# First tile in 256-column halves, weight sums spread over later tiles, four marks moved from ScalarE to VectorE

## The chip, the cores and the metric

The kernel runs on one core of a Trainium2 chip. The metric is the device time of one execution in microseconds; three executions of the kernel before took 225.99, 226.69 and 230.72 us, so the median is 226.69 us. A difference of 2% of that is 4.5 us.

Five engines work side by side, each through its own list of instructions in a fixed order: TensorE (PE for the matmuls, PEld for the weight load that goes ahead of each matmul), VectorE (DVE), ScalarE (ACT), GpSimd (POOL) and SyncE (SP), which issues nearly all DMAs.

## The reference

A recurrent attention with a decaying state, followed by a bilinear feed-forward layer:

```
for t in range(S):
    state = gamma * state + einsum('bhd,bhe->bhde', k[:, :, t], v[:, :, t])
    y[:, :, t] = scale * einsum('bhd,bhde->bhe', q[:, :, t], state)
x = y.transpose(0, 2, 1, 3).reshape(B * S, H * D)
out = ((x @ w_a) * (x @ w_b)) @ w_out
```

B = 4, H = 8, S = 768, D = 64, so there are 3072 tokens of 512 channels; w_a and w_b are 512 x 1536, w_out is 1536 x 512. All inputs and the output are float32; the kernel multiplies in bfloat16 and sums in float32.

## The kernel before

The 3072 tokens are 24 slots of 128 tokens. TILES = [4, 2, 2, 2, 2, 4, 4, 4] groups them into eight tiles J = 0 to 7 of 512 or 256 tokens for the feed-forward part. For each tile there are twelve blocks ft = 0 to 11, one for each 128 of the 1536 hidden channels: `ffn_a` (L574) multiplies x by w_a in four matmuls (kt = 0 to 3) into a PSUM bank, ScalarE copies it to `asb` (L586), `ffn_g` (L588) does the same with w_b, and VectorE multiplies the two into `ht` (L597). A matmul of a block is as wide as the tile, 512 or 256 columns, except where `parts` (L568) cuts it into two halves. The three PSUM banks of the pool psff (tag "ff") go round among a, g, the outputs o and one half of the state products.

Then comes the output product. For J below 5, `ffn_out` (L621) does one 128-token slot i in twelve matmuls of 512 columns, and ScalarE copies the bank to `osb` (L634). For J = 5, 6, 7, `ffn_fast` (L667) does two slots at once with seven products of six 256-column matmuls in place of eight; it needs sums of w_out's quarters (`wt_bf`, made once for each sixth j of w_out by `combine_o`, L213: four VectorE instructions and a ScalarE cast, L217 to L221) and sums of ht's quarters (`hsum`, made by VectorE in `add`, L644, as the blocks go by).

The attention of slots 0 to 5 is done at the start. That of slots 6 to 23 is put in between as visits, by the table `ahead` (L815): at (J, ft) ahead of a block, or at (J, "o", i) ahead of an output product. A visit `turn(new, old)` (L397) does, on TensorE, the first half of `inter` for the old pair of slots (y from the carried state, L360), the chunk states of the new pair (L288), their scores (L318), the second half of `inter`, and `intra` (y from the masked scores, L372). That is up to 128 small matmuls of 64 columns, each with a weight load, so up to 256 instructions. `casts(t)` (L247) scales k and q of a slot on POOL, turns them with a DMA transpose into kqT, and asks for the loads of later slots. VectorE adds the chunk states to running sums (L302) and masks the scores (L324); ScalarE casts the sums to `gst` and, later, y to `xt` (L387).

Between the two halves of `inter` stands a mark: `fenced` (L335) puts a tiny copy of one column on an engine, which waits for the last matmul of the first half; the matmuls that write the same bank's other rows wait for the mark (`into`, L341). In the kernel before the mark of every turn is on ScalarE.

The order of each engine's list is the order in which the code is written (`seq` ties each instruction to the one before it on its engine). No planner changes it. The code of TensorE's list is itself brought onto the core while the kernel runs, in packets that the trace shows on a DMA queue of its own (q8).

Of the kernel before, what the change touches and what calls it, by code (L numbers as in the profile page):

```python
# [24 lines left out]
def kernel(  # L25
# [10 lines left out]
    nc = tc.nc  # L36
# [7 lines left out]
    NFT = DFF // P  # L44
# [288 lines left out]
    fence = {}  # L333
# [60 lines left out]
                seq(nc.vector.tensor_tensor(dst[:, s, on], src[:, s, on], part[:, s], op=ALU.add))  # L394
                seq(nc.vector.tensor_copy(dst[:, s, off], src[:, s, off]))

    def turn(new, old):  # L397
        catch_up()
        apart = None
        if old is not None:  # L400
            ys[old] = [psat.tile([P, 2, KT, D], F32, tag=f"y{c}", name="y") for c in range(2)]
            if new is None:
                both = psat.tile([P, 2, 2, KT, D], F32, tag="at", name="apart")
                apart = [both[:, c] for c in range(2)]
            inter(old, True, ys[old] if new is not None else apart)
# [168 lines left out]
    def ffn_a(J, ft, c0=0, c1=None):  # L574
        c1 = TILES[J] * P if c1 is None else c1
        if J not in ht:
            ht[J] = htp.tile([P, NFT, 4 * P], BF16, tag="ht", name="ht")
        fs = slice(ft * P, (ft + 1) * P)
        a = psff.tile([P, 4 * P], F32, tag="ff", name="a")[:, : c1 - c0]
        for kt in range(KT):  # L580
            for b0, b1 in parts(J, ft, c0, c1, 5):
                seq(nc.tensor.matmul(a[:, b0 - c0 : b1 - c0], wa_bf[:, kt, fs], xcols(J, kt, b0, b1),  # L582
                                     start=(kt == 0 and b0 == c0), stop=(kt == KT - 1 and b1 == c1),
                                     skip_group_check=True))
        asb = asbs[J, ft, c0] = asbp.tile([P, 4 * P], BF16, tag="asb", name="asb")[:, : c1 - c0]
        seq(nc.scalar.copy(asb, a))  # L586

    def ffn_g(J, ft, c0=0, c1=None):  # L588
        c1 = TILES[J] * P if c1 is None else c1
        fs = slice(ft * P, (ft + 1) * P)  # L590
        g = psff.tile([P, 4 * P], F32, tag="ff", name="g")[:, : c1 - c0]
        for kt in range(KT):
            for b0, b1 in parts(J, ft, c0, c1, 5):
                seq(nc.tensor.matmul(g[:, b0 - c0 : b1 - c0], wb_bf[:, kt, fs], xcols(J, kt, b0, b1),  # L594
                                     start=(kt == 0 and b0 == c0), stop=(kt == KT - 1 and b1 == c1),
                                     skip_group_check=True))
# [216 lines left out]
    for j in range(NO):  # L813
# [5 lines left out]
        (1, "o", 1): [(turn, 8, 6), (casts, 10)],  # L819
# [3 lines left out]
        (4, "o", 1): [(turn, 16, 14), (casts, 19)], (5, 0): [(casts, 20)],  # L823
        (5, 2): [(casts, 21)], (5, 8): [(turn, 18, 16), (casts, 22)],
        (5, "o", 2): [(turn, 20, 18), (casts, 23)],
# [63 lines left out]
```

## Time and profile before

| what | value |
|---|---|
| executions | 225.99, 226.69, 230.72 us, median 226.69 |
| the profiled execution's own time | 226.69 us |
| its span | 225.0 us (the other 1.69 us lie around it) |
| TensorE matmuls | busy 214.5 us, 95% of the span, 2717 of them |
| weight loads | busy 140.6 us |
| VectorE, ScalarE, GpSimd | busy 128.7, 98.0 and 81.8 us |
| granted TensorE clock | 0.997 on the mean of the span |
| idle of TensorE put down to "issue" | 1.4 us once (L631) and 1.7 us once (L664) |

TensorE's busy time is an overlapped one: matmuls are pipelined, a 512-column matmul is listed with 379 ns and a 256-column one with 273 ns, while four of 512 columns follow each other in 0.86 us. The chain of waits shows the pace, since it counts each piece only until the next one starts. "issue" in a view means that an engine stood still while nothing that the profile shows was being waited for.

### The profile page before, as it was taken

What the parts mean: (1) busy time and instruction counts of PE and PEld (TensorE: products, weight loads), DVE (VectorE), ACT (ScalarE), POOL (GpSimd) and SP (SyncE); (2) the same over time, 40 slices, a digit from 0 to 9 for tenths busy, and PEclk for the clock granted to TensorE, in tenths of its full rate; (3) what the DMA queues carried; (4) which work ended last, traced back from release to release, by engine and by line L of the source; (5) the groups of instructions that cost most, each with busy time, mean ns of one, the idle gap of its engine ahead of it and who ended that gap; (6) DMA issues with size and microseconds to landing.
All of it is one profiled execution on the core that took longest, in us unless ns stands there. A gap on an engine that the chain in (4) does not pass through costs nothing.

```text
span 225.0 us, 6583 instructions
## 1 busy us (share of the span) xinstructions
PE 214.5 (95%) x2717; PEld 140.6 (62%) x2717; DVE 128.7 (57%) x282; ACT 98.0 (44%) x225; POOL 81.8 (36%) x107
## 2 busy tenths in 40 slices
PE   8799999999999999997999999996999999999993
PEld 7578645784557867864885445476545478444582
DVE  2783547649895434470467267974457793256641
ACT  3674253443656426452447432724435442333331
POOL 6567798573653535161443526161000000000000
PEclk9999999999999999999999999999999999999998
DMA  6999999896998899999948987797200002200022
GB/s 180 345 379 382 365 317 407 249 213 141 217 251 183 224 210 188 212 170 249 215 102 200 212 199 164 170 272 170 93 0 4 0 3 96 93 0 1 3 93 93
DMA packets 94829, 39.74 MB, mean 177 GB/s; under 512 B 76112, under 2 KB 91728, under 8 KB 94800
## 3 DMA queue, kind: packets, MB, share of 16 engines
q1 hardware_dynamic: 94656, 39.20, 68.4%
q8 instruction: 21, 0.34, 0.6%
q10 hardware_dynamic: 144, 0.13, 0.2%
q14 instruction: 8, 0.07, 0.1%
HBM read 28.31 MB, written 6.29 MB: 154 GB/s over the span
## 4 chain that ended last, share of the span: by engine, by line
PE 79%; DMA 7%; issue 3%; DVE 3%; ACT 2%; POOL 2%; SPq 2%; DVEq 0%; ACTq 0%; POOLq 0%
PE a L582 25%; PE g L594 25%; PE o L664 12%; PE o L631 10%; DMA qf<-in_q_dram 4%; DMA vf<-in_v_dram 2%; POOL kqb L240 2%; DMA kqT<-kqb 1%; PE y L360 1%; DVE ht L597 1%; PE y L372 1%; PE at L318 1%; DVE hsum L654 1%; PE tp L440 1%; PE y L519 1%
## 5 line engine op out<-in xcount | busy, mean ns | idle before, releaser
L597 DVE TENSOR_TENSOR ht<-g,asb 128x256 bf16<-128x256 f32 (+1 forms) x98 | 53.9, 550 | 67.2 <-PE g L594 52.6
L594 PE MATMUL g<-xt,wb_bf 128*128 128x256 bf16 (+1 forms) x404 | 77.8, 318 | 0.2 <-ACT asb L586 0.2
L582 PE MATMUL a<-xt,wa_bf 128*128 128x256 bf16 (+1 forms) x404 | 77.5, 318 | 0.1
L586 ACT CAST asb<-a 128x256 bf16<-128x256 f32 (+1 forms) x98 | 46.2, 472 | 66.5 <-PE a L582 65.2
L594 PEld LDWEIGHTS <-wb_bf 128*128 128x128 bf16 x404 | 39.4, 98 | 22.9 <-issue 0.5
L582 PEld LDWEIGHTS <-wa_bf 128*128 128x128 bf16 x404 | 39.2, 98 | 22.7 <-DVE xt L201 0.4
L240 POOL TENSOR_TENSOR kqb<-kf,ktab 128x512 bf16<-128x512 f32 x21 | 22.5, 1072 | 39.9 <-DMA kf<-in_k_dram 36.2
L631 PE MATMUL o<-wo_bf,ht 128*128 128x512 bf16 x144 | 32.6, 379 | 1.4 <-issue 1.4
L240 POOL TENSOR_TENSOR kqb<-qf,qtab 128x512 bf16<-128x512 f32 x21 | 22.7, 1084 | 5.9 <-DMA qf<-in_q_dram 5.8
L631 PEld LDWEIGHTS <-ht 128*128 128x128 bf16 x144 | 13.6, 98 | 17.0 <-issue 1.7
L201 POOL CAST vb<-vf 128x512 bf16<-128x512 f32 x24 | 15.3, 646 | 17.0 <-DMA vf<-in_v_dram 7.5
L302 DVE TENSOR_TENSOR sums<-st,sums 128x256 f32<-128x256 f32 x30 | 12.7, 424 | 5.6 <-PE st L288 4.3
L664 PEld LDWEIGHTS <-hsum 128*128 128x128 bf16 x144 | 14.0, 98 | 2.1 <-DVE hsum L654 0.4
L634 ACT COPY osb<-o 128x512 f32<-128x512 f32 x12 | 7.0, 586 | 15.2 <-PE o L631 12.2
L664 PE MATMUL o<-wt_bf,hsum 128*128 128x256 bf16 x108 | 12.9, 273 | 0.2 <-DVE hsum L654 0.2
L664 PEld LDWEIGHTS <-ht 128*128 128x128 bf16 x108 | 10.4, 97 | 4.3 <-issue 1.9
L199 ACT CAST gst<-sums 128x256 bf16<-128x256 f32 x33 | 11.8, 412 | 0.1
L324 DVE TENSOR_TENSOR aT<-at,mask 128x512 bf16<-128x512 f32 x18 | 11.8, 680 | 0.0
L664 PE MATMUL o<-wo_bf,ht 128*128 128x256 bf16 x72 | 9.1, 273 | 1.7 <-issue 1.7
L387 ACT CAST xt<-y 128x512 bf16<-128x512 f32 x16 | 8.6, 592 | 4.2 <-PE y L372 4.2
L654 DVE TENSOR_TENSOR hsum<-ht 128x512 bf16<-128x512 bf16 (+1 forms) x24 | 9.1, 391 | 0.2
L201 POOL CAST wo_bf<-wsto 128x1024 bf16<-128x1024 f32 x6 | 6.2, 1040 | 3.2 <-DMA wsto<-in_moe_w_out_dram 3.2
(85 smaller groups left out, 171.1 us busy)
## 6 DMA issues: line engine op xcount, KB each, us to landing
out_dram<-osb SPq DMA_DIRECT2D x11, 512.0 KB, 3.2
kf<-in_k_dram SPq DMA_DIRECT2D x18, 256.0 KB, 4.0
qf<-in_q_dram SPq DMA_DIRECT2D x36, 128.0 KB, 3.9
vf<-in_v_dram SPq DMA_DIRECT2D x18, 256.0 KB, 4.3
wsta<-in_moe_w_a_dram SPq DMA_DIRECT2D x6, 512.0 KB, 7.6
wstb<-in_moe_w_b_dram SPq DMA_DIRECT2D x6, 512.0 KB, 7.9
wsto<-in_moe_w_out_dram SPq DMA_DIRECT2D x6, 512.0 KB, 9.0
kf<-in_k_dram SPq DMA_DIRECT2D x3, 512.0 KB, 6.2
```

The source lines that it names most:

```text
L199: seq(nc.scalar.copy(dst, src))
L201: seq(engine.tensor_copy(dst, src))
L240: seq(eng.tensor_tensor(dst, src, tab, op=ALU.mult))
L302: seq(nc.vector.tensor_tensor(new, u[c][:, s], old, op=ALU.add))
L324: unmasked.append(lambda r=r: seq(nc.vector.tensor_tensor(aT[n][:, r].rearrange("p s h d -> p (s h) d"), at[:, r].rearrange("p s h d -> p ...
L582: seq(nc.tensor.matmul(a[:, b0 - c0 : b1 - c0], wa_bf[:, kt, fs], xcols(J, kt, b0, b1), start=(kt == 0 and b0 == c0), stop=(kt == KT - 1 a ...
L586: seq(nc.scalar.copy(asb, a))
L594: seq(nc.tensor.matmul(g[:, b0 - c0 : b1 - c0], wb_bf[:, kt, fs], xcols(J, kt, b0, b1), start=(kt == 0 and b0 == c0), stop=(kt == KT - 1 a ...
L597: seq(nc.vector.tensor_tensor(ht[J][:, ft, c0:c1], g, asbs.pop((J, ft, c0)), op=ALU.mult))
L631: seq(nc.tensor.matmul(o, ht[J][:, ft, i * P : (i + 1) * P], wo_bf[:, f, 2 * r : 2 * r + 2, :].rearrange("p a d -> p (a d)"), start=(ft == ...
L654: seq(nc.vector.tensor_tensor(s[which], x(), y(), op=op))
L664: seq(nc.tensor.matmul(R[:, :DH], lhs, (wo_bf, wt_bf)[w][:, f, m, :], start=(first and f == 0), stop=(f == NH - 1), skip_group_check=True))
```

## The change

Four things are changed.

1. `parts` is called with NFT (12) in place of 5. In tile 0 the blocks 2 to 4 were in 256-column halves before; now blocks 2 to 11 are. This makes 7 blocks x 2 products x 4 = 56 more matmuls and as many weight loads, 112 more TensorE instructions, all ahead of the first visit. TensorE's list has 5,548 rows now in place of 5,436.
2. `combine_o` of the six parts of w_out stood after the output products (0,0) twice, (0,1), (0,2), (0,3) and (1,0); now it stands after (0,0), (0,1), (0,2), (0,3), (2,0) and (3,1).
3. The mark of the turns 8, 10, 16 and 20 is on VectorE in place of ScalarE.
4. Turn 22 stands ahead of block (6, 8) in place of (6, 6).

```
-            for b0, b1 in parts(J, ft, c0, c1, 5):
+            for b0, b1 in parts(J, ft, c0, c1, NFT):          (in ffn_a and in ffn_g)
...
-    def turn(new, old):
+    def turn(new, old, eng=nc.scalar):
...
-                fence[old, 0] = fence[old, 1] = fenced(nc.scalar)
+                fence[old, 0] = fence[old, 1] = fenced(eng)
...
-        (2, 2): [(casts, 11)], (2, 7): [(casts, 12)], (2, "o", 1): [(turn, 10, 8), (casts, 13)],
+        (2, 2): [(casts, 11)], (2, 7): [(casts, 12)], (2, "o", 1): [(turn, 10, 8, D_), (casts, 13)],
...
-        (6, 6): [(turn, 22, 20)], (6, "o", 0): [(turn, None, 22)],
+        (6, 8): [(turn, 22, 20)], (6, "o", 0): [(turn, None, 22)],
...
-    combined = {(0, 0): (0, 1), (0, 1): (2,), (0, 2): (3,), (0, 3): (4,), (1, 0): (5,)}
+    combined = {(0, 0): (0,), (0, 1): (1,), (0, 2): (2,), (0, 3): (3,), (2, 0): (4,), (3, 1): (5,)}
```

Three places show what moves. The first is TensorE's list around row 4,025 (counted from 0). Before, the last matmul of the second-last product of the first `ffn_fast` of tile 5 and the first instructions of turn 20 stand there (rows 4,021 to 4,025; o is the output bank, ht the hidden values, y the attention output, gst the carried state):

```order
L664 LDWEIGHTS ht_2792
L664 MATMUL o_3147<-wt_bf_175,ht_2792 128x256
L360 LDWEIGHTS gst5_161
L360 MATMUL y_3200<-kqT_2587,gst5_161 64x64
L360 LDWEIGHTS gst5_161
```

In the changed kernel the rows 4,025 to 4,029 are the end of an a product and the start of a g product in a block of tile 5:

```order
L582 LDWEIGHTS wa_bf_172
L582 MATMUL a_3164<-xt_2646,wa_bf_172 128x512
L594 LDWEIGHTS wb_bf_173
L594 MATMUL g_3171<-xt_2646,wb_bf_173 128x512
L594 LDWEIGHTS wb_bf_173
```

From the first visit on every instruction stands 112 rows further down the list; turn 22 has in addition changed places with the blocks 6 and 7 of tile 6 (32 rows). Counted in rows, the turns 12, 14, 16, 18 and 20 start at 2,467, 2,963, 3,227, 3,619 and 4,023 before, and at 2,579, 3,075, 3,339, 3,731 and 4,135 now. Nine rows of either list, the same nine places, wait for two semaphores at once.

The second place is VectorE's list from turn 8 to turn 10 (mark is the mark, sums the running state sums, aT the masked scores, the four rows L217 to L220 one `combine_o`; -: before, +: now):

```order
+L337 COPY mark<-bq 128x1
+L302 TENSOR_TENSOR sums<-st,sums 128x256 x4
+L324 TENSOR_TENSOR aT<-at,mask 128x512 x2
+L597 TENSOR_TENSOR ht<-g,asb 128x256 x12
 L217 TENSOR_TENSOR tmp<-wsto 128x256
 L218 TENSOR_TENSOR tmp<-wsto,tmp 128x256
 L219 TENSOR_TENSOR wt_bf<-wsto 128x256
 L220 TENSOR_TENSOR wt_bf<-wsto,tmp 128x256
-L302 TENSOR_TENSOR sums<-st,sums 128x256 x4
-L324 TENSOR_TENSOR aT<-at,mask 128x512 x2
-L597 TENSOR_TENSOR ht<-g,asb 128x256 x12
+L337 COPY mark<-bq 128x1
```

One `combine_o` that stood ahead of turn 8's work stands after the blocks of tile 2 now, directly ahead of turn 10's mark, and both marks are new in this list.

The third place is ScalarE's list at the end of tile 3, from the last cast of turn 12's sums over the two output copies (osb) to the copies of tile 4's blocks (asb):

```order
 L199 CAST gst_160<-sums 128x256
 L634 COPY osb<-o 128x512 x2
+L221 CAST wt_bf<-tmp 128x512
 L586 CAST asb<-a 128x256 x12
```

A `combine_o` cast stands between the last output copy of tile 3 and the first copy of tile 4 now.

More of the change, by code (lines that the diff above doesn't have):

```diff
@@ L580, in ffn_a @@
         for kt in range(KT):
-            for b0, b1 in parts(J, ft, c0, c1, 5):
+            for b0, b1 in parts(J, ft, c0, c1, NFT):
                 seq(nc.tensor.matmul(a[:, b0 - c0 : b1 - c0], wa_bf[:, kt, fs], xcols(J, kt, b0, b1),
@@ L592, in ffn_g @@
         for kt in range(KT):
-            for b0, b1 in parts(J, ft, c0, c1, 5):
+            for b0, b1 in parts(J, ft, c0, c1, NFT):
                 seq(nc.tensor.matmul(g[:, b0 - c0 : b1 - c0], wb_bf[:, kt, fs], xcols(J, kt, b0, b1),
@@ L818 @@
         (0, "o", 3): [(casts, 9, "kq"), (casts, 8, "v"), (casts, 9, "v")],
-        (1, "o", 1): [(turn, 8, 6), (casts, 10)],
-        (2, 2): [(casts, 11)], (2, 7): [(casts, 12)], (2, "o", 1): [(turn, 10, 8), (casts, 13)],
+        (1, "o", 1): [(turn, 8, 6, D_), (casts, 10)],
+        (2, 2): [(casts, 11)], (2, 7): [(casts, 12)], (2, "o", 1): [(turn, 10, 8, D_), (casts, 13)],
         (3, 0): [(casts, 14)], (3, 6): [(casts, 15)], (3, "o", 0): [(turn, 12, 10), (casts, 16)],
         (4, 0): [(casts, 17)], (4, "o", 0): [(turn, 14, 12), (casts, 18)],
-        (4, "o", 1): [(turn, 16, 14), (casts, 19)], (5, 0): [(casts, 20)],
+        (4, "o", 1): [(turn, 16, 14, D_), (casts, 19)], (5, 0): [(casts, 20)],
         (5, 2): [(casts, 21)], (5, 8): [(turn, 18, 16), (casts, 22)],
-        (5, "o", 2): [(turn, 20, 18), (casts, 23)],
-        (6, 6): [(turn, 22, 20)], (6, "o", 0): [(turn, None, 22)],
+        (5, "o", 2): [(turn, 20, 18, D_), (casts, 23)],
+        (6, 8): [(turn, 22, 20)], (6, "o", 0): [(turn, None, 22)],
     }
```

## The prediction

> **What bounds the kernel now.** I read the page first, then the chain of waits, then who TensorE waited for, then the timeline around the waits. From the page:
>
> ```profile
> span 225.0 us, 6583 instructions
> PE 214.5 (95%) x2717; PEld 140.6 (62%) x2717; DVE 128.7 (57%) x282; ACT 98.0 (44%) x225; POOL 81.8 (36%) x107
> ```
>
> TensorE is the bound: an edit counts only where it removes or makes a wait of TensorE, or changes its pace. The pace stands in the chain of waits, in pieces counted to the start of the next:
>
> ```profile
> 19.66 1.75 PE a L582 x16
> 30.44 0.86 PE a L582 x4
> ...
> 98.79 2.48 PE o L631 x11
> 101.27 1.41 issue
> ...
> 151.41 0.21 PE y L360 x10
> ...
> 152.63 0.98 PE o L664 x8
> 153.61 1.69 issue
> ```
>
> Halves go at 1.75 / 16 = 0.1094 us each, full matmuls at 0.86 / 4 = 0.215. And there are two pieces in which TensorE does nothing, named "issue": 1.41 and 1.69 us, together 3.10 us. The waits of TensorE name them as its two longest, with nothing else above 1.1 us:
>
> ```profile
> PE o L664 <- issue: 1.7, 1, 1.7
> PE o L631 <- issue: 1.4, 1, 1.4
> PE tp L440 <- DVE kqb L240: 1.1, 4, 0.4
> ...
> PE at L318 <- DMA kqT<-kqb: 0.2, 1, 0.2
> ```
>
> What "issue" is here: the page has a queue of 21 packets, 0.34 MB, so 16 KB each. TensorE's 2717 matmuls and 2717 weight loads make 5,434 instructions, 5,434 / 21 = 259 per packet. The first gap ends at row 2,747 of TensorE's list, the second at row 4,281; the list in between holds two rows that wait for two semaphores and so take an extra wait instruction each, and 1,534 + 2 = 1,536 = 6 x 256. So code comes in pages of 256 instructions, and both gaps end exactly at a page's first instruction. In both a page packet was on its way shortly before:
>
> ```profile
> q8 instruction: 21, 0.34, 0.6%
> q8 instruction: 1, 0.02, 13.4%
> q8 instruction: 1, 0.02, 5.8%
> 97.30 0.32 PE L360 MATMUL y<-kqT,gst 64*64 64x64 bf16 x16
> 98.29 0.51 PE L372 MATMUL y<-aT,vb 64*64 64x64 bf16 x32
> 102.69 2.97 PE L631 MATMUL o<-wo_bf,ht 128*128 128x512 bf16 x13 [1.41 <-issue]
> 155.30 0.60 PE L664 MATMUL o<-wo_bf,ht 128*128 128x256 bf16 x4 [1.69 <-issue]
> ```
>
> (The second and third rows are the windows 99 to 99.5 and 152.5 to 153.7 us.) A turn runs its 256 instructions from 97.30 to about 98.7 us, 5.6 ns each, against 0.1094 / 2 = 55 ns in a block. I read it so: when TensorE enters a page, the one after it is asked for; where a page starts at the beginning of a turn, it is used up too fast. In turn 12 a page starts 25 rows in (row 2,492), in turn 20 2 rows in (row 4,025), by 256 rows back from the gaps. These points are at about 97.4 us (the first of the turn's rows at 97.30 covers 32) and 151.4 us (the row of turn 20's first matmuls). To the ends of the gaps at 102.69 and 155.30 are 5.3 and 3.9 us: a next page takes that long.
>
> [...]
>
> **The change part by part.** The sum is made against the profiled execution, 226.69 us (span 225.0 us and 1.69 around it), which is also the median of the runs.
>
> *112 more instructions ahead of the visits.* All page starts fall 112 rows earlier in the work. I counted them through the changed list. Turn 12 now has a page start 168 rows in, turn 20 146 in, and before the next page over 160 rows of blocks or products follow the turn: at 55 ns that is 8.8 us against 5.3. Both gaps go: -1.41 - 1.69 = **-3.10**. What is late next there: nothing that the waits of TensorE name before the marks below.
>
> New short pages: the shortest distances of the changed list, timed by today's trace over the same work, are turn 14 to turn 16 (a page start near the beginning of `intra` in both), turn 18 into the blocks behind it (5.0 us), and tile 4's blocks into turn 14 (5.0 us). For the first:
>
> ```profile
> 116.90 0.50 PE L372 MATMUL y<-aT,vb 64*64 64x64 bf16 x31
> 121.05 0.46 PE L372 MATMUL y<-aT,vb 64*64 64x64 bf16 x32
> 116.20 0.44 PE L288 MATMUL st<-vb,kqb 64*64 64x64 bf16 x30
> 120.02 0.32 PE L360 MATMUL y<-kqT,gst 64*64 64x64 bf16 x16
> ```
>
> 121.05 - 116.90 = 4.15 us. In the kernel before, the page that starts in the L288 row (116.2) had its next one start at the end of the L360 row of turn 16 (16 matmuls from 120.02, some 0.13 us), 3.9 us later, and no "issue" wait of TensorE stands there. So a page takes between under 3.9 and 5.3 us: a wait of 0 to 1.15 us at turn 16, 0 to 0.3 at each of the two others. I take 0.5 for the three, nearer the pages without a wait: **+0.50** (0 to 1.75).
>
> *The halves themselves.* One a or g product is 8 x 0.1094 = 0.875 us in place of 0.86, times 14 = +0.21 us. The weight loads are hidden as they are in the row at 19.66 us, which is the same shape. Behind it, turn 8 waits for a transpose in any case:
>
> ```profile
> 62.80 3.29 DMA kqT<-kqb
> ...
> 66.13 0.32 PE at L318 x16
> ```
>
> The transpose lands at 62.80 + 3.29 = 66.09 us and the scores start then; a later start of TensorE is taken up there, if the DMA does not move. I take **+0.10** (0 to 0.21).
>
> *Marks on VectorE.* In the turns 10 and 16 TensorE waits for ScalarE's mark, which is queued behind an output copy:
>
> ```profile
> 83.59 0.21 PEld L360 LDWEIGHTS <-gst 64*64 64x64 bf16 x16 [0.17 <-ACT mark L337]
> 120.90 0.21 PEld L360 LDWEIGHTS <-gst 64*64 64x64 bf16 x16 [0.17 <-ACT mark L337]
> 80.30 0.42 DVE L597 TENSOR_TENSOR ht<-g,asb 128x256 bf16<-128x256 f32 x1 [0.45 <-PE g L594]
> 83.32 1.34 DVE L302 TENSOR_TENSOR sums<-st,sums 128x256 f32<-128x256 f32 x3 [2.60 <-PE st L288]
> ```
>
> Both go: **-0.34**. Queued behind the mark on VectorE are the sums, which wait for TensorE's later matmuls anyway. In turn 10 a `combine_o` (next rows) stands ahead of the mark: 0.506 + 0.642 + 0.415 + 0.484 = 2.05 us, inside the 2.60 us in which VectorE is idle: from 80.30 + 0.42 = 80.72 to 82.77, half a microsecond ahead of the sums at 83.32. If that cover is gone, TensorE waits for what is over. Turn 8 is held by the transpose, turn 20 shows no wait for its mark: 0 each.
>
> *Weight sums spread.* Work that leaves tiles 0 and 1 gains nothing, since no wait of TensorE names VectorE or ScalarE there. What arrives: the two `combine_o` at tiles 2 and 3.
>
> ```profile
> L217 DVE TENSOR_TENSOR tmp<-wsto 128x256 f32<-128x256 f32 x6 | 3.0, 506 | 0.0
> L218 DVE TENSOR_TENSOR tmp<-wsto,tmp 128x256 f32<-128x256 f32 x6 | 3.9, 642 | 0.2
> L219 DVE TENSOR_TENSOR wt_bf<-wsto 128x256 bf16<-128x256 f32 x6 | 2.5, 415 | 0.0
> L220 DVE TENSOR_TENSOR wt_bf<-wsto,tmp 128x256 bf16<-128x256 f32 x6 | 2.9, 484 | 0.0
> L221 ACT CAST wt_bf<-tmp 128x512 bf16<-128x512 f32 x6 | 3.6, 620 | 0.5 <-DVE tmp L218 0.4
> 105.69 0.59 ACT L634 COPY osb<-o 128x512 f32<-128x512 f32 x1 [2.00 <-PE o L631]
> 106.18 0.37 ACT L586 CAST asb<-a 128x256 bf16<-128x256 f32 x1
> 106.80 0.60 PE L594 MATMUL g<-xt,wb_bf 128*128 128x256 bf16 x4
> ```
>
> At the end of tile 3 ScalarE goes from the output copy straight to the first copy of tile 4, 106.18 to 106.55 us. The cast of 0.62 us now goes between (about 0.5 in a row of overlapping instructions), so that copy ends near 107.1. The fourth product of tile 4 (106.80) takes the bank that this copy frees, and waits about 0.3 us: **+0.30** (0 to 0.6). At (2,0) the cast stands ahead of a turn and a 2.7 us output product, which hide it. No DMA moves: SyncE's list is the same.
>
> *Turn 22 two blocks later.* VectorE has fewer blocks for its sums and masks before tile 6's hsum are due. The same place in tile 5 has one more sum, and cost TensorE this:
>
> ```profile
> 148.42 1.59 PE L664 MATMUL o<-wt_bf,hsum 128*128 128x256 bf16 x13 [0.17 <-DVE hsum L654]
> ```
>
> In tile 6 the last turn's matmuls and two products stand ahead, so I take **+0.10** (0 to 0.3).
>
> Sum: -3.10 + 0.50 + 0.10 - 0.34 + 0.30 + 0.10 = -2.44; 226.69 - 2.44 = 224.25, so **224.2 us**, 1.1% faster. That is inside 2%, about what a measurement of this kernel can tell from no change.
>
> **The rivals.**
>
> *The gaps come back elsewhere* (0.20). All three short pages take the 5.3 us of turn 12: 1.75 in place of 0.50, 225.5 us. For it: turn 12 did take that long. Against: the page of 3.9 us without a wait at the same place.
>
> *The gaps are not the code's* (0.08) but belong to the products in which they stand: then they stay, and -2.44 + 3.10 = +0.66, 227.3 us. For it: the profile only says "issue". [...] Against: the 1,536 instructions between them, and that only one of the 12 output products of L631 and one of the six fast ones has such a gap.
>
> *The weight loads of the halves stand open* (0.05), the side slower than before. 56 more loads, listed with 98 ns each:
>
> ```profile
> L582 PEld LDWEIGHTS <-wa_bf 128*128 128x128 bf16 x404 | 39.2, 98 | 22.7 <-DVE xt L201 0.4
> ```
>
> If all of it showed, 56 x 0.098 = 5.5 us, 224.2 + 5.5 = 229.7 us; it is slower than before from 2.44 / 56 = 44 ns a load on. It would be in tile 0, from 30 to 48 us. Against: 16 halves in 1.75 us, where an open load would give 16 x 0.2 = 3.3.
>
> *More is gained* (0.07): no short page waits, ScalarE's cast is hidden and the halves are free: -3.10 - 0.34 = -3.44, 223.25, and with the fastest of the three runs of before, 0.70 below the median, as the scatter, 222.6 us.
>
> **How the numbers follow.** My forecast has 0.60; its own range is 223.3 to 225.2 (its terms at their near ends). The range to hold 8 in 10 takes in the gain at its fullest with scatter, 222.6, and the short pages with ScalarE's wait at its full 0.6 and 0.7 of scatter, 225.5 + 0.3 + 0.7 = 226.5. Over 2% faster is under 222.2 us: 0.04, from the last rival. Over 2% slower is over 231.2 us: 0.02, beyond even the open loads. Within 2%: 0.94.
>
> **What would show it.** No "issue" piece over 0.3 us in the chain at the output product behind turn 12 or in the first fast product behind turn 20; the page packets 112 rows earlier. Any new "issue" piece stands in turn 16, within 40 rows behind turn 18 or in turn 14, and at a page's first row. Tile 0's blocks at 1.75 us for 16 halves. No wait for a mark in turns 10 and 16. A wait of some 0.3 us at tile 4's fourth product. I am wrong if the two gaps stay at their products, if a gap of over 1.2 us stands elsewhere, or if TensorE begins to wait for kqT in turn 16.

## The result and the profile after

The changed kernel took 224.44 us at the median of 20 executions, the kernel before 226.47 us at the median of 20 executions beside it. The ratio is 0.9913, with a 95% interval of 0.9884 to 0.9941: 0.9% faster, within the 2% that count as no change. The profiled execution of the changed kernel took 223.94 us with a span of 222.2 us; that of before 226.69 and 225.0 us.

From the page of the changed kernel, the span, the busy time of the engines, and the queue that brings TensorE's code:

```profile
span 222.2 us, 6684 instructions
...
PE 212.8 (96%) x2764; PEld 145.5 (65%) x2773; DVE 129.8 (58%) x286; ACT 97.3 (44%) x221; POOL 81.9 (37%) x107
...
q8 instruction: 21, 0.34, 0.6%
```

56 more weight loads are listed (2,773 in place of 2,717), and still the span is 2.8 us shorter. Whom TensorE waited for in the changed kernel (us in total, times, longest):

```profile
PE tp L440 <- DVE kqb L240: 1.8, 3, 1.4
...
PE o L631 <- issue: 0.6, 4, 0.2
PE y L360 <- issue: 0.6, 1, 0.6
...
PE y L360 <- DVE mark L337: 0.3, 1, 0.3
```

The two rows of before with 1.7 us (L664) and 1.4 us (L631) are gone; what is left of "issue" at L631 is four short waits of at most 0.2 us. A new "issue" of 0.6 us stands in a turn (y, L360), and so does a wait for a mark on VectorE. The chain of waits of the changed kernel shows the same at two of the places. Each row is a start, a length up to the next step, and what ran:

```profile
98.71 5.14 PE o L631 x23
...
119.34 0.15 PE y L360 x15
119.49 0.56 issue
120.06 0.21 PE y L360
```

The third place, the first fast product behind turn 20, stands in the timeline (start, length, engine and line, operation; an idle time ahead of a row would stand behind it in brackets):

```profile
151.47 1.49 PE L664 MATMUL o<-wo_bf,ht 128*128 128x256 bf16 x12
152.79 2.33 PE L664 MATMUL o<-wt_bf,hsum 128*128 128x256 bf16 x18
```

The first row of the chain is the pair of output products behind turn 12: 5.14 us without a break, where before a piece of 1.41 us stood behind the eleventh matmul. 23 matmuls are on record there, but 24 weight loads (nine matmul records are missing from this trace), so the pace is 5.14 / 24 = 0.214 us each, that of full matmuls. The other rows of the chain are turn 16, with the new gap behind the fifteenth matmul. In the fast product 12 matmuls are followed by 18 without a bracket, where before 1.69 us of "issue" stood behind the eighth.

Since the order of TensorE's list is fixed, the starts of its weight loads can be put beside each other stage by stage. This table is worked out from them, each stage counted from its first weight load to that of the next stage:

| stage | before, us | after, us | difference | predicted |
|---|---|---|---|---|
| start to the first visit (tile 0, the first products) | 55.55 | 55.61 | +0.06 | +0.10 |
| turn 8 | 2.02 | 1.55 | -0.47 | 0 |
| turn 10 | 1.41 | 1.70 | +0.29 | -0.17 |
| turn 12 | 1.42 | 1.30 | -0.12 | 0 |
| the two products behind turn 12 | 6.55 | 4.98 | -1.57 | -1.41 |
| tile 4's blocks | 10.79 | 11.10 | +0.31 | +0.30 |
| turn 16 | 1.41 | 1.93 | +0.52 | +0.50 - 0.17 |
| tile 5 from turn 18 to turn 20 | 12.12 | 12.01 | -0.11 | 0 |
| product behind turn 20 | 6.43 | 4.79 | -1.64 | -1.69 |
| tile 6 with turn 22 | 22.22 | 22.21 | -0.01 | +0.10 |
| sum | | | -2.74 | -2.44 |

All other stages agree to 0.02 us. The first row holds the start, which scatters by 0.7 us between profiles (the part up to the first block took 14.74 to 15.48 us). So the sum came out nearly as predicted, with two terms wrong, turn 8 by -0.47 and turn 10 by +0.46, that cancel.

**Turn 8.** The timeline of the kernel before, at turn 8 (start, length, engine and line, operation, and in brackets the idle time ahead of it):

```profile
65.67 0.62 ACT L221 CAST wt_bf<-tmp 128x512 bf16<-128x512 f32 x1
...
66.13 0.21 PEld L318 LDWEIGHTS <-kqT 64*64 64x64 bf16 x16 [0.34 <-DMA kqT<-kqb]
...
66.19 0.18 ACT L337 COPY mark<-bq 128x1 f32<-128x1 f32 x1
...
66.43 0.17 PEld L360 LDWEIGHTS <-gst 64*64 64x64 bf16 x10
```

and of the changed kernel:

```profile
65.36 0.15 DVE L337 COPY mark<-bq 128x1 f32<-128x1 f32 x1
...
65.88 0.21 PEld L318 LDWEIGHTS <-kqT 64*64 64x64 bf16 x16 [0.23 <-DMA kqT<-kqb]
...
66.00 0.15 PEld L360 LDWEIGHTS <-gst 64*64 64x64 bf16 x8
```

and its transpose in the chain:

```profile
62.34 3.49 DMA kqT<-kqb
```

Before, two things come together: the transpose, for which the second half of the scores waits (66.13), and the mark, which stands on ScalarE behind the cast of a `combine_o` (66.19 to 66.37). The second half of `inter` starts at 66.43, 0.30 us behind these scores and right behind the mark, so the mark is the last of the two. After, the mark is there long before the scores (65.36), and `inter` starts 0.12 us behind them. That is 0.18 us of the 0.47. The transpose lands earlier too, at 62.34 + 3.49 = 65.83 us against 66.09; counted from the start of the turn, which is 0.07 us later now, the scores behind it start 0.32 us earlier.

**Turn 10.** The timeline of the changed kernel on VectorE, GpSimd and TensorE's loads:

```profile
80.23 0.41 DVE L217 TENSOR_TENSOR tmp<-wsto 128x256 f32<-128x256 f32 x1
80.42 1.14 POOL L240 TENSOR_TENSOR kqb<-kf,ktab 128x512 bf16<-128x512 f32 x1 [4.08 <-DMA kf<-in_k_dram]
80.68 1.15 DVE L218 TENSOR_TENSOR tmp<-wsto,tmp 128x256 f32<-128x256 f32 x1
...
81.75 0.41 DVE L219 TENSOR_TENSOR wt_bf<-wsto 128x256 bf16<-128x256 f32 x1
81.76 1.31 POOL L240 TENSOR_TENSOR kqb<-qf,qtab 128x512 bf16<-128x512 f32 x1 [0.21 <-DMA qf<-in_q_dram]
82.09 1.26 DVE L220 TENSOR_TENSOR wt_bf<-wsto,tmp 128x256 bf16<-128x256 f32 x1
83.27 0.14 DVE L337 COPY mark<-bq 128x1 f32<-128x1 f32 x1
...
83.47 0.21 PEld L360 LDWEIGHTS <-gst 64*64 64x64 bf16 x16 [0.46 <-DVE mark L337]
```

`combine_o` begins right behind the last ht, as the prediction had it, but runs from 80.23 to 82.09 + 1.26 = 83.35 us, 3.12 us in place of 2.05. Two of its four instructions run beside GpSimd's scaling of k and q (`casts`) and end 0.27 and 0.28 us behind it: 80.68 + 1.15 = 81.83 against 80.42 + 1.14 = 81.56, and 83.35 against 81.76 + 1.31 = 83.07. So the mark behind it is late and TensorE's loads stand 0.46 us.

In both meetings GpSimd's instruction was running when VectorE's began (80.42 against 80.68 us, 81.76 against 82.09). Where VectorE's was running first (80.23 and 81.75), it kept its 0.41 us and GpSimd's took 1.14 and 1.31 us, against 1.04 in 34 of the 42 rows of that kind in this profile. So by these rows the one that began second was held up, and both times VectorE ended less than one instruction of its own (0.41 us) behind GpSimd; what the two share is not shown.

**Tile 4.** The chain of the changed kernel at the end of tile 3, and the row of the fourth product:

```profile
103.88 0.45 ACT osb L634
104.36 0.62 ACT wt_bf L221
104.98 0.28 ACT asb L586
```
```profile
105.30 0.60 PE L594 MATMUL g<-xt,wb_bf 128*128 128x256 bf16 x4 [0.15 <-ACT asb L586]
```

The cast stands between the last output copy and the first `asb`, as predicted, and the blocks are 0.31 us longer.

### The profile page after: what moved, and what is told of

It reads as the page before. It is cut to its first block, busy times and chain, and to the rows that moved or that the text cites. A ratio compares the mean times of both kernels' runs of the same rounds, so it can differ in the third digit from the quotient of the medians.

```text
span 222.2 us, 6684 instructions
## 1 busy us (share of the span) xinstructions
PE 212.8 (96%) x2764; PEld 145.5 (65%) x2773; DVE 129.8 (58%) x286; ACT 97.3 (44%) x221; POOL 81.9 (37%) x107
## 4 chain that ended last, share of the span: by engine, by line
PE 84%; DMA 6%; ACT 3%; DVE 2%; POOL 1%; issue 1%; SPq 1%; POOLq 0%; DVEq 0%
PE a L582 28%; PE g L594 28%; PE o L664 12%; PE o L631 9%; DMA kf<-in_k_dram 3%; DMA vf<-in_v_dram 2%; DMA kqT<-kqb 2%; PE y L360 1%; POOL kqb L240 1%; PE y L372 1%; PE at L318 1%; PE y L519 1%; PE st L288 1%; PE tp L440 1%; DVE wt_bf L220 1%
## 5 line engine op out<-in xcount | busy, mean ns | idle before, releaser
L594 PEld LDWEIGHTS <-wb_bf 128*128 128x128 bf16 x432 | 42.1, 98 | 20.6 <-issue 0.3
L582 PEld LDWEIGHTS <-wa_bf 128*128 128x128 bf16 x432 | 41.8, 98 | 20.8 <-DVE sums L302 0.5
L631 PE MATMUL o<-wo_bf,ht 128*128 128x512 bf16 x136 | 31.3, 380 | 0.8 <-issue 0.6
L631 PEld LDWEIGHTS <-ht 128*128 128x128 bf16 x144 | 13.6, 98 | 15.4
L664 PEld LDWEIGHTS <-hsum 128*128 128x128 bf16 x144 | 14.0, 98 | 2.1 <-DVE hsum L654 0.2
L664 PE MATMUL o<-wt_bf,hsum 128*128 128x256 bf16 x108 | 13.1, 273 | 0.0
L664 PEld LDWEIGHTS <-ht 128*128 128x128 bf16 x108 | 10.4, 97 | 2.3
L664 PE MATMUL o<-wo_bf,ht 128*128 128x256 bf16 x72 | 8.9, 273 | 0.0
```

Source lines behind the costliest of these rows:

```text
L631: seq(nc.tensor.matmul(o, ht[J][:, ft, i * P : (i + 1) * P], wo_bf[:, f, 2 * r : 2 * r + 2, :].rearrange("p a d -> p (a d)"), start=(ft == ...
L664: seq(nc.tensor.matmul(R[:, :DH], lhs, (wo_bf, wt_bf)[w][:, f, m, :], start=(first and f == 0), stop=(f == NH - 1), skip_group_check=True))
```

## The experiments

The theory: TensorE's code comes in pages of 256 instructions; a gap arises where a page is used up before the next one is there; 112 instructions more in the list move the pages out of turns 12 and 20. The main rival: the gaps belong to the products, or to the work that the change moves (marks, sums), and not to the position in the list. The terms of the sum that came out otherwise (turns 8 and 10) and the new gap in turn 16 are the second question.

The readings below rest on one table, worked out like the one above from the starts of the weight loads in each profile (us). "Behind turn 12" is the two output products there, "behind turn 20" the rest of tile 5's first pair of slots, and "tile 5" is from turn 18 to turn 20: the last blocks and the first half of the fast products.

| kernel | turn 8 | turn 10 | behind turn 12 | tile 4's blocks | turn 16 | tile 5 | behind turn 20 |
|---|---|---|---|---|---|---|---|
| before | 2.02 | 1.41 | 6.55 | 10.79 | 1.41 | 12.12 | 6.43 |
| halves alone | 2.37 | 1.41 | 4.98 | 10.79 | 1.78 | 13.37 | 4.79 |
| all but the halves | 1.55 | 1.22 | 5.71 | 11.10 | 1.55 | 11.96 | 5.47 |
| 112 rows of other work | 1.44 | 1.41 | 4.98 | 10.79 | 1.45 | 12.91 | 4.79 |
| 48 rows | 1.91 | 1.41 | 4.98 | 10.79 | 2.21 | 12.07 | 4.79 |
| marks alone | 3.08 | 1.31 | 5.38 | 10.78 | 1.22 | 12.33 | 5.47 |
| after | 1.55 | 1.70 | 4.98 | 11.10 | 1.93 | 12.01 | 4.79 |
| after, again | 1.27 | 1.22 | 4.98 | 11.10 | 1.91 | 12.74 | 4.79 |
| after, turn 22 back | 1.35 | 1.22 | 4.98 | 11.10 | 1.34 | 13.08 | 4.79 |
| after, sums placed otherwise | 1.27 | 1.22 | 4.98 | 10.79 | 2.06 | 11.96 | 4.79 |
| the same, marks on ScalarE | 1.39 | 1.41 | 4.98 | 10.79 | 1.77 | 11.69 | 4.79 |
| the same, turn 14 earlier | 1.39 | 1.22 | 4.98 | 10.71 | 1.35 | 12.97 | 4.79 |

The column "tile 5" goes up and down by 1.7 us whatever the kernel; the first experiment shows one way in which it comes about.

### The halves alone

```
-            for b0, b1 in parts(J, ft, c0, c1, 5):
+            for b0, b1 in parts(J, ft, c0, c1, NFT):
```

> Only the first part: tile 0's blocks 2 to 11 in halves, marks, weight sums and turn 22 as before. Pages of code (theory): all page starts are where the changed kernel has them, so the gaps of 1.41 and 1.69 us behind the turns 12 and 20 are gone; a gap of 0.3 to 1 us is in turn 16 (page of some 4.2 us), and one of 0 to 1.5 us may come at the end of turn 22, which at its old place has a page of 3.7 us. Sum -3.1 + 0.6 + 0.5 + 0.1: about 224.8 us, 224.0 to 225.6. Rival, the gaps belong to the products they stand in: both stay, 226.8 us. Rival, marks and sums make the gain: 226.8 us, with gaps moved but not shorter in sum.

Measured: 224.86 us, ratio 0.9983 (0.9952 to 1.0013); the profile's span is 223.2 us. Both gaps are gone (6.55 to 4.98, 6.43 to 4.79), so the halves alone carry the term of -3.10. The ratio is nearly 1 all the same. In the profile two waits take part of it back: at turn 8 the mark behind ScalarE's cast (the transpose was issued 1.6 us earlier than in the profile of before, 61.19 against 62.80 us, and is no longer waited for), and in tile 5 the sums of ht. Whom TensorE waited for in this kernel, and its timeline at the end of tile 5's blocks:

```profile
PE y L360 <- ACT mark L337: 1.0, 1, 1.0
...
PE o L664 <- DVE hsum L654: 0.6, 1, 0.6
```
```profile
146.64 1.09 POOL L240 TENSOR_TENSOR kqb<-kf,ktab 128x512 bf16<-128x512 f32 x1
146.75 2.17 DVE L654 TENSOR_TENSOR hsum<-ht 128x256 bf16<-128x256 bf16 x2
...
147.69 1.08 POOL L240 TENSOR_TENSOR kqb<-qf,qtab 128x512 bf16<-128x512 f32 x1
...
148.98 0.28 PE L664 MATMUL o<-wt_bf,hsum 128*128 128x256 bf16 x1 [0.61 <-DVE hsum L654]
```

Two hsum take 2.17 us beside two GpSimd instructions, where a pair takes 0.48 to 0.49 us elsewhere. It is the collision of turn 10 again. GpSimd's scaling waits for the loads of k and q (4.08 us in the row at 80.42 above), so where it meets VectorE can differ from one profile to the next, and the stage does: 13.37 here, 13.08 and 12.97 in two versions of the changed kernel, 11.69 in another.

### All but the halves

The changed kernel, with the halves as before:

```
-            for b0, b1 in parts(J, ft, c0, c1, NFT):
+            for b0, b1 in parts(J, ft, c0, c1, 5):
```

> The changed kernel without its first part: halves only in the blocks 2 to 4, as before; marks, weight sums and turn 22 as changed. Pages of code: the gaps are back at rows 2,747 and 4,281 with 1.2 to 1.9 us each, none in turn 16; marks and sums give -0.5 to +0.3: about 226.6 us. Rival, marks and sums make the gain: 224.6 us.

Measured: 224.92 us, ratio 0.9997 (0.9963 to 1.003). The gaps are back, at the rows of the list at which they stand before. The timeline of this kernel on TensorE:

```profile
101.06 1.24 PE L631 MATMUL o<-wo_bf,ht 128*128 128x512 bf16 x5 [0.57 <-DVE tmp L217]
...
153.11 0.60 PE L664 MATMUL o<-wo_bf,ht 128*128 128x256 bf16 x4 [0.73 <-issue]
```

The first one is put down to a VectorE instruction that ended at about that time, but an output product does not read what that writes, and the row is the first of a page: 2,747 in the list, as before. The gaps are smaller than in the profile of before (5.71 - 4.98 = 0.73 and 5.47 - 4.79 = 0.68, against 1.57 and 1.64). Turn 10 is 0.19 us shorter and tile 4 0.31 longer, as the marks and the cast should make them. A third, small gap was not expected: turn 16 takes 1.55 us, against 1.22 with the marks alone, and the break is at the first row of a page.

By the ratios the two parts apart give 0.2% together, and the whole change 0.9% (0.7% when it was timed again, below). Each interval is 0.3% to either side, so much of the difference can be scatter; whether anything more is in it stays open.

### 112 rows that are not halves

```
+    def spin(n):
+        idle = psff.tile([P, 4 * P], F32, tag="ff", name="spin")
+        for i in range(n):
+            seq(nc.tensor.matmul(idle[half(i % 2), :D], zero[half(0), :D], zero[half(0), :D],
+                                 start=True, stop=True, skip_group_check=True))
...
-        (1, "o", 1): [(turn, 8, 6), (casts, 10)],
+        (1, "o", 1): [(spin, 56), (turn, 8, 6), (casts, 10)],
```

Nothing else is changed against the kernel before: 56 small matmuls on zeros, whose result nobody reads, lengthen the list by 112 rows ahead of turn 8.

> The kernel before with 112 more TensorE instructions of another kind: 56 matmuls of 64 columns on zeros with their weight loads, some 0.75 us in all, ahead of turn 8, where TensorE waits 0.5 us for a transpose; no halves, nothing else changed. Their sums are used nowhere. Pages of code: the gaps behind the turns 12 and 20 are gone as with the halves, a gap of 0.3 to 1 us in turn 16, 0 to 1.5 us in turn 22: 226.7 - 3.1 + 1.1 + 0.3 = 225.0 us. Rival, narrower matmuls make the gain: 227.2 us, both gaps in place.

Measured: 224.04 us, ratio 0.9956 (0.9927 to 0.9985): a little faster than before, with 0.88 us of useless matmuls added (the stage of the 56). Turn 8 is short here (1.44 us) because it starts behind these matmuls, when the transpose and the mark are nearly there: they come 0.74 and 0.80 us into the turn, against 1.17 and 1.46 us before. Both gaps are gone, with 4.98 and 4.79 us to the hundredth as with the halves. The timeline of this kernel behind turn 12 (24 weight loads, one matmul record is missing):

```profile
98.37 5.13 PE L631 MATMUL o<-wo_bf,ht 128*128 128x512 bf16 x23 [0.16 <-issue]
```

It is the position in the list that counts, not what the matmuls of tile 0 are like.

### 48 rows

The kernel before, with three blocks more in halves:

```
-            for b0, b1 in parts(J, ft, c0, c1, 5):
+            for b0, b1 in parts(J, ft, c0, c1, 8):
```

> The kernel before with halves in the blocks 2 to 7: 48 rows more in place of 112. Pages of code: short pages of 2.8 us behind turn 14, 3.0 us in turn 12, 3.7 us in turn 16 and 4.1 us in turn 20, against some 4.5 us that a page takes: gaps of about 1.7, 1.5, 0.8 and 0.4 us there, 4.4 in sum against 3.1 before, so slower: 227.9 us (226.5 to 229). None in the output product behind turn 12 nor in the first fast product behind turn 20. Rival, narrower matmuls make the gain: 3/7 of it, 225.8 us. Rival, the gaps belong to their products: 226.8 us, same places.

Measured: 225.11 us, ratio 1.0011 (0.9973 to 1.0049). The timeline of this kernel in turn 12 and in turn 16:

```profile
98.92 0.29 PE L372 MATMUL y<-aT,vb 64*64 64x64 bf16 x13 [0.98 <-issue]
...
121.02 0.21 PE L372 MATMUL y<-aT,vb 64*64 64x64 bf16 x1 [0.59 <-issue]
```

The gaps move with the pages, into turn 12 (2.44 in place of 1.42 us) and turn 16; that is what only the theory of pages gives. But their sum is 1.6 us, and not the 4.4 us that were expected, since none stands behind turns 14 and 20. The packets of q8, put beside the starts of the pages, show why. In turn 12 and turn 20 of before the next page's packet started 1.91 and 1.21 us after TensorE had entered a page; in turn 14 here, where the page starts among blocks, at 55 ns an instruction, it started 0.12 us ahead of that, and behind turn 20 0.30 us after it. So the list can be read ahead, and a time that is counted from the moment at which TensorE enters a page is too long there. It is not a fixed lead: over the profiles, the packet that follows a page starting among blocks or output products came from 2.0 us ahead of that start to 2.7 us behind it.

### The changed kernel again, and with the sums placed otherwise

The first ran unchanged; the second differs from it in one line:

```
-    combined = {(0, 0): (0,), (0, 1): (1,), (0, 2): (2,), (0, 3): (3,), (2, 0): (4,), (3, 1): (5,)}
+    combined = {(0, 0): (0, 1), (0, 1): (2,), (0, 2): (3,), (0, 3): (4,), (3, 0): (5,)}
```

Only the sixth part stands elsewhere than in the kernel before, behind output product (3, 0), where another output product covers ScalarE's cast.

> The changed kernel once more, so that it is measured on the same chip and against the same runs of the kernel before as the next one. Expected: no gap behind the turns 12 and 20, one of 0 to 0.6 us in turn 16; a wait of some 0.4 us for the mark of turn 10, since two of the four weight-sum instructions ahead of it run into POOL's kqb (1.15 and 1.26 us in place of 0.64 and 0.48), and 0.3 us at tile 4's fourth product: 224.2 us.

> The changed kernel with its weight sums at other places: two after the output product (0,0), then one each after (0,1), (0,2), (0,3), and the last after (3,0), so that none stands directly ahead of turn 10's mark or between tile 3's last output copy and tile 4's first copy. TensorE's list is the same row by row, so the pages are the same. If the two waits are what the moved sums cost: neither wait is left, 0.46 + 0.31 = 0.8 us less than the changed kernel, 223.5 us. Rival, the waits come from VectorE being behind in any case: no difference, 224.2 us.

Measured: 223.63 us, ratio 0.9929 (0.9895 to 0.9964) for the changed kernel again, and 222.84 us, ratio 0.9899 (0.9844 to 0.9954) with the sums placed otherwise. Tile 4's blocks are back at 10.79 us, so the 0.31 us were the cast. For the rest of the 0.79 us the profiles name nothing that the edit does, and the intervals overlap: "after, again" had no wait at turn 10 either. Its timeline there:

```profile
80.25 0.42 DVE L218 TENSOR_TENSOR tmp<-wsto,tmp 128x256 f32<-128x256 f32 x1
80.60 1.27 DVE L219 TENSOR_TENSOR wt_bf<-wsto 128x256 bf16<-128x256 f32 x1
81.79 0.41 DVE L220 TENSOR_TENSOR wt_bf<-wsto,tmp 128x256 bf16<-128x256 f32 x1
82.25 0.15 DVE L337 COPY mark<-bq 128x1 f32<-128x1 f32 x1
```

Here one instruction of the four begins behind one of GpSimd's and takes 1.27 us, and the mark is in time; in the profile of after two of them did (1.15 and 1.26), and the cover was gone. So the wait at turn 10 is there in one of the four profiles with this order on VectorE (after, after again, turn 22 back, all but the halves), and the gain of 0.19 us in the three others.

### The marks alone

The kernel before, with the marks of turns 8, 10, 16 and 20 on VectorE:

```
-                fence[old, 0] = fence[old, 1] = fenced(nc.scalar)
+                fence[old, 0] = fence[old, 1] = fenced(eng)
...
+        (1, "o", 1): [(turn, 8, 6, D_), (casts, 10)],           (and so at turns 10, 16 and 20)
```

> The kernel before with only the four marks on VectorE; TensorE's rows stand where they did. Marks worth what the changed kernel shows in turn 8 (0.48 us) and what the page of waits says in the turns 10 and 16 (0.17 each): those three turns 0.8 us shorter in sum, both page gaps in place, 225.9 us where the kernel before takes 226.7. By the prediction's own term, 0.34 us and turn 8 unchanged.

Measured: 225.04 us, ratio 1.0009 (0.9971 to 1.0047). Turns 10 and 16 are shorter by 0.10 and 0.19 us, but turn 8 takes 3.08 us in place of 2.02. The timeline of this kernel at turn 8, and then its engines by stretches (start and end; length, busy time of PE, PEld, DVE, ACT and POOL with counts; the granted clock; DMA share and GB/s):

```profile
66.96 0.28 PE L360 MATMUL y<-kqT,gst 64*64 64x64 bf16 x10 [0.54 <-DVE mark L337]
```
```profile
65.00:67.00 2.00, 0.85 (x52) 0.62 (x53) 1.97 (x7) 0.76 (x2) 0.11 (x1) 1.00 0.97 219
67.50:71.30 3.80, 3.80 (x16) 1.36 (x11) 2.31 (x5) 2.29 (x6) 2.09 (x2) 0.55 1.04 234
```

The `combine_o` that is still in that place stands ahead of the mark on VectorE. TensorE is busy 0.85 of 2 us there, and then it is granted only 0.55 of its clock for the output product: 4.08 us in place of 2.39. This profile is of an execution of 226.64 us, against a median of 225.04, and the only one of the ten with a granted clock of 0.992 on the mean; the other nine had 0.997 or more. So the slow product is that execution's, and how long turn 8 was in the others is not known. In this profile the marks need the sums out of the way at turn 8.

### The marks back on ScalarE, sums placed otherwise; the control beside it

The version with the sums placed otherwise, with the mark of every turn on ScalarE; that version itself ran again on the same chip.

```
-        (1, "o", 1): [(turn, 8, 6, D_), (casts, 10)],
+        (1, "o", 1): [(turn, 8, 6), (casts, 10)],               (and so at turns 10, 16 and 20)
```

> As e8 with all marks on ScalarE again. What the marks on VectorE are worth when no weight sum stands ahead of them: the turns 8, 10 and 16 some 0.45, 0.2 and 0.15 us longer, 0.7 to 0.8 us in sum. By the prediction's term, 0.34 us.

> The changed kernel with the weight sums at the other places, once more, on the chip of the next two: some 0.8 us under the changed kernel's ratio of 0.993 to the kernel before, so 0.989 to 0.990, with one page gap of 0.1 to 1 us left, in turn 16.

Measured: 222.9 us, ratio 0.9887 (0.9826 to 0.9947), against 223.23 us, ratio 0.989 (0.9858 to 0.9922), for the control. There is no difference to be measured. By the stages, turn 8 is 0.12 us longer than in the profile of the version with the sums placed otherwise and turn 10 0.19, as the marks should make it, and turn 16 is 0.29 shorter: there the gap is the page's, which scatters, and it hides the mark on either engine. So by the profiles the marks are worth 0.31 us at turns 8 and 10, and nothing at turn 16 while the gap is there.

### Turn 14 earlier, against the gap in turn 16

```
-        (4, 0): [(casts, 17)], (4, "o", 0): [(turn, 14, 12), (casts, 18)],
+        (4, 0): [(casts, 17)], (4, 4): [(turn, 14, 12)], (4, "o", 0): [(casts, 18)],
```

This is made against the version with the sums placed otherwise. The new gap of turn 16 comes from a page that starts in turn 14 and is used up by turn 16; with turn 14 ahead of block (4, 4), 6.9 us of tile 4's blocks and an output product lie between the two turns.

> As e8, and turn 14 stands ahead of block (4, 4) in place of behind the blocks of tile 4, so that 128 rows of blocks lie between it and the place it had. Pages of code: no page start is left in turn 16's neighbourhood that has to follow another within 4.8 us (the shortest page is 4.9 us, from turn 14 into the blocks behind it), so the last gap, in turn 16, goes: 0.1 to 0.9 us less than e8. Turn 14's own work costs the same at either place. Rival, the wait in turn 16 is for its inputs and not for code: no change, or a wait for turn 14's transposes at its earlier place makes it slower.

Measured: 222.48 us, ratio 0.9876 (0.9815 to 0.9936), 0.75 us under the control. Turn 16 takes 1.35 us in place of 2.06 and no "issue" wait of it is left. By its ratio to the kernel before it is the fastest of all that ran, and ahead of the changed kernel (0.9913). Against the control the intervals overlap, so the times alone would not tell. The 0.71 us are gone from the profile, and the page ahead of turn 16's lasts 6.7 us there, longer than any page that was waited for. But one profile is not much: in the next experiment the same gap was missing once with the rows of the changed kernel. So that the move removes the gap is likely, and not shown.

### Turn 22 back at (6, 6)

The changed kernel, with:

```
-        (6, 8): [(turn, 22, 20)], (6, "o", 0): [(turn, None, 22)],
+        (6, 6): [(turn, 22, 20)], (6, "o", 0): [(turn, None, 22)],
```

> The changed kernel with turn 22 ahead of block (6, 6) again. Counted by the time of the work the page that starts ahead of it there lasts 3.3 to 3.7 us, against 3.1 to 3.7 us that a page takes while the DMA queues are idle, counted from a page start inside a run of small matmuls; but where a page starts in a block its packet starts up to 2 us before TensorE gets there. So no gap in turn 22 and no change, 0 to -0.1 us. Rival: a gap of 0.5 us or more at the end of turn 22.

One execution: 223.29 us. Turn 22 stands without a gap here too: its page's successor was on its way 1.91 us ahead of the page's start, which lies in a block. Tile 6 with turn 22 takes 22.21 or 22.22 us in all profiles, at either place, so in the profiles moving the turn neither cost nor gained. Turn 16, whose rows are the same as in the changed kernel, had no gap in this profile (1.34 us): the page took 3.88 us there, against 4.79 us in the version with the sums placed otherwise. The gap is the page's time, and that scatters.

### How long a page takes

```
+        (2, 4): [(spin, 384)], (7, 4): [(spin, 384)],
```

The kernel before, with 384 small matmuls as above (three pages) at a place with much DMA traffic and at one with almost none.

> The kernel before with two runs of 384 matmuls of 64 columns on zeros (768 rows, three pages each) that nobody uses: one in tile 2 ahead of block 4, while loads are on the queues, one in tile 7 ahead of block 4, where the DMA queues are idle. It measures what a page takes. At some 13 ns each they would last 5 us. Pages of code: in each two pages in a row wait for their code, and from page start to page start it takes 3.9 to 5.3 us in tile 2 and some 3.4 us in tile 7 (0.9 to the packet, 1.1 for it, 1.4 until it is used); gaps at page starts alone. 243 us in all. Rival, TensorE's small matmuls are slow by themselves or the gaps have nothing to do with pages: no gaps at page starts, 236 us.

One execution: 250.73 us. The timeline on TensorE at the first place (tile 2), then at the second one (tile 7), and the stretches:

```profile
73.22 3.16 PE L818 MATMUL spin<-zero 64*64 64x64 bf16 x188
79.18 3.62 PE L818 MATMUL spin<-zero 64*64 64x64 bf16 x128 [2.80 <-issue]
83.46 2.02 PE L818 MATMUL spin<-zero 64*64 64x64 bf16 x68 [0.66 <-issue]
...
214.55 5.16 PE L818 MATMUL spin<-zero 64*64 64x64 bf16 x174 [0.92 <-issue]
```
```profile
72.00:75.00 3.00, 3.00 (x124) 2.69 (x124) 0.93 (x3) 0.75 (x2) 1.42 (x2) 1.00 0.89 272
...
79.20:84.00 4.80, 4.14 (x149) 4.01 (x150) 0.00 (x0) 0.00 (x0) 1.28 (x2) 0.50 0.83 187
...
215.00:219.00 4.00, 3.90 (x148) 3.76 (x142) 0.00 (x0) 0.00 (x0) 0.00 (x0) 0.50 0.02 4
```

Between the two gaps stand exactly 128 matmuls with 128 loads: a page of 256 instructions, seen directly. From page to page go 5.02 and 4.28 us at the first place, at a DMA share of 0.83 to 0.99, and 3.14 and 3.73 us at the second, at 0.02. The expectation of 243 us did not reckon with the clock, which is 0.50 behind the gaps: there a row of 128 matmuls took 3.62 us, 28 ns each, against 3.16 / 188 = 17 ns in the first row.

This run says one thing more. 384 matmuls are 768 rows, three whole pages, so behind them the pages start at the same work as in the kernel before. Of its two gaps one is there and one is not; the timeline behind turn 12, then behind turn 20:

```profile
116.24 2.96 PE L631 MATMUL o<-wo_bf,ht 128*128 128x512 bf16 x13 [1.31 <-issue]
...
167.41 2.34 PE L664 MATMUL o<-wt_bf,hsum 128*128 128x256 bf16 x18
```

The first stands behind the eleventh matmul again (the stage takes 6.45 us). Behind turn 20 the products go on without a bracket (4.79 us), although the page is used up in 2.1 us: its successor's packet started at 164.26 us, 0.61 us ahead of the page, and not 1.21 us behind it as in the kernel before. So a page start at a bad place makes a gap possible, and not certain.

## Why the prediction was right, and where it was wrong

**Right: the gaps are the code's, and 112 rows take them away.** -3.10 was predicted, -3.21 measured in the profile (1.57 + 1.64). Three kernels bear it out: the rows alone do it, whatever is computed in them; without them the gaps return to the same rows; with 48 they go elsewhere. The rival that the gaps belong to their products has fallen. The size of the term is another matter. The median moved by 2.0 us and the profile by 2.8. The four profiles with the old position of the pages (before, all but the halves, marks alone, and the test with 384 matmuls) have 1.57, 0.73, 0.40 and 1.47 us behind turn 12 and 1.64, 0.68, 0.68 and 0 behind turn 20: 1.79 us together on the mean, and not 3.1. So the one execution on which the sum was made had the largest gaps of the four. That smaller ones are common would account for the 0.8 us, but was not measured for the kernel before itself, and on the times alone the halves by themselves gained nothing that is clear of noise (0.9952 to 1.0013).

A page start among the blocks of tile 4 showed no gap: they take 10.78 or 10.79 us in all seven profiles in which no turn and no cast is put among them, with a page start among them (the halves alone, 10.79) or without one (before, 10.79). In and behind turns and in rows of small matmuls 0.4 to 2.8 us were lost where a page was waited for, by the rows above.

**Right: short pages, +0.50.** The gap came in turn 16, as named, and measured 0.56 us as "issue". The stage grew by 0.52, not by 0.33: where the mark frees TensorE earlier, TensorE only waits longer for the page, so -0.17 at turn 16 did not come. The rival in which all three pages take the 5.3 us of turn 12 did not come true; the step "so a page takes between under 3.9 and 5.3 us" held at its upper end; the pages that were waited for took 2.99 to 5.30 us over all profiles.

**Right: ScalarE's cast at tile 4, +0.30.** 0.31 us in all four profiles with the cast there, and 0.00 in the others. The halves: +0.06 against +0.10, with a scatter of the start that is larger than both.

**Wrong: "If that cover is gone" at turn 10.** The step was 0.506 + 0.642 + 0.415 + 0.484 = 2.05 us, "inside the 2.60 us in which VectorE is idle". The means hid that these instructions take 0.41 to 0.43 us alone and up to 1.27 us where they begin behind one of GpSimd's scaling (1.15 and 1.26 in the profile of after). With one such meeting the sum fits (1.27, the changed kernel again), with two it is 3.12 us and does not. So -0.17 became +0.29 in the profile and -0.19 in three others.

**Wrong: "Work that leaves tiles 0 and 1 gains nothing" and "Turn 8 is held by the transpose".** The stage gave 0.47 us. The transpose is the wait that the view names in the profile of before, but the mark behind the sums' cast ended later (66.37 us against 66.09), and the second half of `inter` followed it. The same holds with the halves alone, where that mark cost 1.0 us, with 48 rows and in the test with 384 matmuls: whenever the transpose landed, from 0.31 to 1.17 us into the turn, `inter` went on 0.05 us behind the mark. With the sums gone from there, turn 8 takes 1.27 to 1.55 us. By the rows above the mark is 0.18 us of the 0.47; the rest is the transpose, earlier. It is issued at 61.19 to 62.80 us in the profiles with the sums in place and at 60.29 to 62.34 us with them moved; whether the move has a part in that or all of it is scatter stays open.

**Too high: turn 22, +0.10.** It measured 0.00.

The two wrong terms, -0.47 + 0.46 = -0.01 against the forecast, cancel, and the largest term had the size of one execution's gaps, so the total was right partly by luck.

## What to carry to other kernels

When the bound engine stands with nothing to wait for, count its instructions between two such gaps; if a multiple of the page comes out (256 here), shift the list (here 112 rows helped and 48 only moved the gaps), so that no page starts at the beginning of a stretch of small matmuls that uses it up before the next one is there (it took 2.99 to 5.30 us here, where it was waited for). Read a gap's size from several profiles before it goes into a sum: here it was 0 to 1.6 us at the same place. Move a mark, and what it queues behind, together: where two waits end within half a microsecond of each other, as at turn 8, freeing one of them shows little. And where instructions of one kind differ in length (0.41 to 1.27 us here), cost a cover with the longest.

## What the hardware showed that was not expected

- Where a page of TensorE's code was waited for, it took 2.99 to 5.30 us from the start of the page before it, and 3.14 and 3.73 us with hardly any DMA traffic. The packet itself takes 0.9 to 1.9 us of that, and 1.2 to 1.6 us, once 2.3, go by between its end and the first instruction. Where the page ahead starts among long matmuls, the packet started from 2.0 us before that page was entered to 2.7 us after.
- VectorE's instructions of `combine_o` and of hsum took 0.28 to 0.43 us alone and as much as 1.27 us where they began behind one of GpSimd's scaling (1.09 us there, 1.04 in most rows); those that write 256 columns of ht from a PSUM bank and `asb` kept their 0.42 us beside GpSimd.
- The granted clock was lower behind some waits. With the marks alone, TensorE was busy 0.85 of the 2 us from 65 to 67, the clock was 0.55 from 67.5 to 71.3, and the product there took 1.69 us longer (in one execution of ten, by its mean clock). In the test with 384 matmuls it was 0.50 behind the gaps of 2.80 and 0.66 us and from 215 us on, behind that of 0.92. Behind the gaps of 1.41 and 1.69 us of before it was 1.00 (102.7 to 104 and 155.3 to 158 us). What decides it is not shown.
